# A decode step with adaptive norms, cached attention and a token mixer: the last eight heads in an order written out step by step

## The chip, the cores and the metric

The kernel runs on one core of a Trainium2 chip. The metric is device time in microseconds (us) of the whole program, the median of several runs. Engines are named as the profile names them: PE is TensorE's matmuls and PEld its weight loads, DVE is VectorE, ACT is ScalarE, POOL is GpSimd, SP is SyncE, which here only issues DMAs. All data is float32.

## The reference, cut to what matters

One token for each of four batch rows goes through an attention block with cached keys and values and then through a token mixer, each behind an adaptive layer norm.

```python
mod = (silu(c) @ w_mod).reshape(4, 6, 1, 512)       # w_mod: 512 x 3072
sa, ca, ga, sb, cb, gb = ...                        # the six blocks of it
h = layernorm(x) * (1 + ca) + sa                    # x: 4 x 1 x 512
q = h @ wq                                          # 32 heads of 128
scores = q @ k.T * 128 ** -0.5                      # 8 key/value heads, 4096 keys, 4 query heads on each
o = softmax(scores) @ v
x = x + ga * (o @ wo)
h = layernorm(x) * (1 + cb) + sb
u = gelu(layernorm(h)[:, :, None] * w1 + b1)        # per channel: 1 -> 1792
x = x + gb * (u @ w2 + b2)                          # 1792 -> 1
```

The keys and values are 4 x 8 x 4096 x 128 each, 67 MB and 67 MB; with the weights about 157 MB are read.

## The kernel before, in words

Work is counted in rounds 0 to 31, one for each pair of batch row and key/value head (round 8b + h). The host has laid out the keys of a round as 128 x 4096 and its values as 128 partitions of 32 rows of 128.

**Loads.** SP issues all loads. A ring of three slots, each with room for two blocks of 2 MB, holds them: `load_pair(i)` brings the keys of round i+2 and the values of round i in one DMA of 4 MB. The last slots are filled block by block: the keys of rounds 30 and 31 (`load_key`), the values of 28 and 29, the values of 30 and 31 in pieces (`load_v`), and at the end the sixth block of `w_mod` (`load_wm5`, L206). A load waits until every reader of what stood in its slot is done.

**A round.** The steps of round i, each with its engine:

- scores (PE, L238): eight products of 32 columns of queries with 512 keys each, into `s`, a PSUM tile of 128 x 1024; then DVE takes the row maximum (L241).
- the maximum over the four row groups: PE turns it (L247), DVE reduces it (L249), PE spreads it (L256), DVE copies it (L258).
- exponential on ACT with row sums (L261).
- transposes: PE turns the exponentials into the same PSUM tile `s` (L268), PE adds the row sums (L272); DVE copies the turned values to `pT` (L276; L274 for round 31) and makes from the sums a selecting matrix (L279, L281).
- values (PE, L292; L302 for round 31): 16 products with 256 value columns each, accumulated in `pv`; DVE copies them (L296, L306).
- project: PE picks the query heads from that copy (L317), DVE copies them (L319), PE multiplies with `wo` (L328 or, for the last batch row, L335), DVE adds to the row's sum (L342, L344). Rounds 30 and 31 add into the tile `pgx` instead.

`s` has two buffers, `pv` one, and one more PSUM pool of two buffers serves every small result in turn (turned maximum, spread maximum, sums, pick, project, gathered statistics): a new one waits until the reader of the one two before it is done.

**The mixer.** When a batch row's eight rounds are done, the class `Mixer` does its second half piecemeal in the next rounds: `residual`, two norms (statistics on DVE, gathered over partitions by PE at L369), `normalise`, then seven pieces each of `expand` (DVE, L405), `gelu` (ACT, L448) and `consume` (PE, L410 or L416). The last batch row's mixer is `finish`, at the end of the program. `fold_gate` multiplies (DVE, L537) two of `wo`'s blocks with the residual's gate so that rounds 30 and 31 can add straight to the residual.

**The order.** The program is given in `manual_schedule`: every engine runs its instructions in the order in which Python emits them, and waits are derived from the tiles. Rounds 0 to 27 come from one loop, in which round i does scores i+2, pick i-1, transposes i+1, project i-1, the maximum i+2, values i in two halves, the exponential i+2 and a part of the mixer. Rounds 28 to 31 follow in straight code (L589 to L639), ending in the residual of the last batch row and `finish`.

Of the kernel before, what the change touches and what calls it, by code (L numbers as in the profile page):

```python
# [19 lines left out]
P = 128  # L20
# [11 lines left out]
def adaln_decode(ctx: ExitStack, tc: tile.TileContext, small, x, wmod, wq, kk, kv, vv, wo, out):  # L32
# [20 lines left out]
    nc.sync.dma_start(sm, small)  # L53
# [177 lines left out]
    S, SEL, SP = {}, {}, {}  # L231

    def scores(i):
        b, h = divmod(i, HKV)
        s = ps_s.tile([P, 1024], F32, name=f"s{i}", tag="s")
        for n in range(2):
            for c in range(4):
                mm(s[32 * c:32 * c + 32, n * 512:(n + 1) * 512], QT[:, b, h, :],  # L238
                   KT[i][:, (n * 4 + c) * 512:(n * 4 + c + 1) * 512], start=True, stop=True)
        m = wk.tile([P, 1], F32, name="m")  # L240
        dv.tensor_reduce(m, s, axis=AX.X, op=OP.max)  # L241
        S[i] = [s, m]

    def colmax(i):
        s, m = S[i]
        pm = ps_m.tile([1, P], F32, name="pm", tag="m")
        nc.tensor.transpose(pm, m, ident)  # L247
        mx = wk.tile([1, 4, 32], F32, name="mx")
        dv.tensor_reduce(mx, pm.rearrange("o (c r) -> o r c", c=4).unsqueeze(1).to_broadcast([1, 4, 32, 4]),  # L249
                         axis=AX.X, op=OP.max)  # L250
        S[i] = [s, mx]

    def expo(i):
        s, mx = S[i]
        pb = ps_m.tile([P, 1], F32, name="pb", tag="m")
        mm(pb, mx.rearrange("o c r -> o (c r)"), neg1, start=True, stop=True)  # L256
        nm = wk.tile([P, 1], F32, name="nm")
        dv.tensor_copy(nm, pb)  # L258
        p = wk.tile([P, 1024], F32, name="p", tag="p")
        l = wk.tile([P, 1], F32, name="l")  # L260
        nc.scalar.activation(p, s, AF.Exp, bias=nm, accum_out=l)  # L261
        S[i] = [s, p, l]

    def transposes(i, then=None):
        s, p, l = S.pop(i)
        pt = s.rearrange("p (k n) -> p k n", k=8)
        for k in range(8):
            nc.tensor.transpose(pt[:, k, :], p[:, k * P:(k + 1) * P], ident)  # L268
        if then:
            then()  # L270
        pl = ps_m.tile([P, 1], F32, name="pl", tag="m")
        mm(pl, grp, l, start=True, stop=True)  # L272
        if i == NS - 1:
            dv.tensor_copy(pTl[:, :, :, 0:REP], pt.rearrange("p k (c r) -> p k c r", c=4)[:, :, :, 0:REP])  # L274
        else:
            dv.tensor_copy(pTs[i % 3][:, :, 0:2 * REP].rearrange("p k (c r) -> p k c r", c=2),  # L276
                           pt.rearrange("p k (h c r) -> p (k h) c r", h=2, c=2)[:, :, :, 0:REP])
        rl = wk.tile([P, 1], F32, name="rl")
        dv.reciprocal(rl, pl)  # L279
# [4 lines left out]
    PV = {}  # L284

    def values(i, ks, pv=None):
        if ks[0] == 0:
            PV[i] = ps_v.tile([P, 2 * DH], F32, name="pv", tag="pv") if pv is None else pv
        pv = PV[i]
        for k in ks:  # L290
            q = k % 4
            mm(pv[32 * q:32 * q + 32, :], pTs[i % 3][:, k, :],  # L292
               VT[i][:, k * 2:(k + 1) * 2, :].rearrange("p j d -> p (j d)"), start=(k < 4), stop=(k >= 12))
        if ks[-1] == 15:
            po = wk.tile([P, 2 * DH], F32, name="po")
            dv.tensor_copy(po, pv)  # L296
            SP[i] = (SEL.pop(i), po)

    def values_last(i, ks, pv):
        for k in ks:  # L300
# [3 lines left out]
        if ks[-1] == 7:  # L304
            po = wk.tile([P, DH], F32, name="po")
            dv.tensor_copy(po, pv)  # L306
            SP[i] = (SEL.pop(i), po)

    ACC = {}
    OT = {}  # L310

    def project_a(i):
        sel, po = SP.pop(i)
        pt = ps_m.tile([P, REP], F32, name="pt", tag="m")
# [3 lines left out]
        oT = wk.tile([P, REP], F32, name="oT")  # L318
        dv.tensor_copy(oT, pt)  # L319
        OT[i] = oT  # L320

    def project_b(i, pa=None):
# [7 lines left out]
        else:  # L330
# [7 lines left out]
            if h >= HKV - 2:  # L338
                return
        if h == 0:  # L340
# [78 lines left out]
    class Mixer:  # L419
# [5 lines left out]

        def residual(self):
            b = self.b
            residual(XK[:, b], fold_groups(ps_e, ACC.pop(b), "e"))
            self.st = stats(XK[:, b], b)

        def modulate(self):
            self.h1, self.st = adaln(self.b, gather(self.st))

        def normalise(self):
            self.hb, self.wr = affine(gather(self.st), bcast(self.h1, self.b))
# [34 lines left out]
        def inner(self, k):  # L470
            self.ripe = len(self.done)
            if k == 0:
# [201 lines left out]
```

## Time and profile before

| | us |
|---|---|
| runs shown | 393.55, 395.03, 395.13 |
| median | 395.03 |
| profiled execution, whole | 393.89 |
| its span, first to last instruction | 392.1 |
| PE busy | 298.3 (76%) |
| DVE busy | 180.3 (46%) |
| ACT busy | 99.6 (25%) |
| time of the load queue's packets, share of 16 DMA engines | 93.6% |
| bytes moved | 157.80 MB |

The busy time of an engine is a sum over stages with different limits. The span has three parts: the prologue (modulation and queries) until the first keys are there, the rounds, and the end behind the last load. Which engine or queue sets the pace is read from each part by itself, by what ended the waits in it.

### The profile page before, as it was taken

The page shows a single profiled execution, that of the slowest core. Times are in us where ns is not written, and L with a number is a line of the kernel's source. Part 1 is how long each engine was busy: PE and PEld are TensorE (multiplying, and loading weights), DVE is VectorE, ACT ScalarE, POOL GpSimd, SP SyncE. Part 2 cuts the span into 40 slices and gives each one's busy share as a digit, 9 for nine tenths or more (in the row PEclk, how much of TensorE's full clock was granted, in tenths as well). Part 3 has the DMA queues.
Part 4 walks back from the last instruction along what each step waited for, and adds up shares of the span by engine and source line. Part 5 has one row for each costly group of instructions (what it writes and reads, how often), then busy time and mean ns, then how long its engine had stood idle before and what let it go on. Part 6 is the DMA issues. An engine that isn't in the chain of part 4 may idle for free.

```text
span 392.1 us, 7228 instructions
## 1 busy us (share of the span) xinstructions
PE 298.3 (76%) x3180; PEld 146.8 (37%) x3180; DVE 180.3 (46%) x491; ACT 99.6 (25%) x123; POOL 0.7 (0%) x6
## 2 busy tenths in 40 slices
PE   0578685913868739978698879998888879899885
PEld 0012142400533305434243325553334225555663
DVE  0620331510433404666365524765555356557766
ACT  1001120110110201114548111145751111465316
POOL 0000000000000000000000000000000000000000
PEclk9989886985998957999899976999999889999997
DMA  8999999999999999999999999999999999999600
GB/s 325 428 431 431 428 453 440 404 448 431 425 431 426 436 426 438 433 440 439 426 431 424 430 435 430 433 428 434 436 435 430 431 430 430 416 425 420 258 3 3
DMA packets 7415, 157.80 MB, mean 402 GB/s; under 512 B 964, under 2 KB 980, under 8 KB 1368
## 3 DMA queue, kind: packets, MB, share of 16 engines
q1 hardware_dynamic: 7376, 157.33, 93.6%
q8 instruction: 25, 0.41, 0.4%
q14 instruction: 6, 0.05, 0.0%
q10 hardware_dynamic: 8, 0.00, 0.0%
HBM read 157.32 MB, written 0.01 MB: 401 GB/s over the span
## 4 chain that ended last, share of the span: by engine, by line
DMA 64%; PE 27%; DVE 6%; ACT 1%; issue 1%; SPq 0%; DVEq 0%
DMA kv<-in_kv 57%; PE s L238 7%; DMA kv<-in_vv 5%; PE pv L292 3%; PE pa L328 3%; PE s L268 3%; PE s L137 2%; PE qs L152 2%; DMA sm<-in_small 2%; PE pt L317 2%; DVE mx L249 1%; PE py L410 1%; DVE acc L344 1%; PE pb L256 1%; PE pm L223 1%
## 5 line engine op out<-in xcount | busy, mean ns | idle before, releaser
L238 PE MATMUL s<-kv,QT 128*32 128x512 f32 x512 | 76.5, 725 | 55.0 <-DMA kv<-in_kv 54.6
L261 ACT ACTIVATE p<-s,nm 128x1024 f32<-128x1024 f32 x32 | 35.7, 1115 | 212.9 <-DVE nm L258 212.8
L241 DVE TENSOR_REDUCE m<-s 128x1 f32<-128x1024 f32 x32 | 39.2, 1225 | 104.9 <-PE s L238 104.8
L292 PE MATMUL pv<-kv,pT 128*32 128x256 f32 x960 | 64.5, 387 | 0.0
L238 PEld LDWEIGHTS s<-kv,QT 128*32 128x32 f32 x512 | 15.6, 123 | 94.8 <-DMA kv<-in_kv 62.4
L268 PE MATMUL s<-ident,p 128*128 128x128 f32 x256 | 36.5, 288 | 0.6 <-ACT p L261 0.6
L268 PEld LDWEIGHTS s<-ident,p 128*128 128x128 f32 x256 | 31.5, 157 | 3.7 <-ACT p L261 1.9
L292 PEld LDWEIGHTS pv<-kv,pT 128*32 128x32 f32 x960 | 25.6, 110 | 15.3 <-issue 0.6
L317 PEld LDWEIGHTS pt<-sel,po 128*128 128x128 f32 x126 | 17.6, 202 | 30.8 <-issue 25.7
L328 PE MATMUL pa<-wo,oT 128*32 128x512 f32 x192 | 27.3, 642 | 0.0
L249 DVE TENSOR_REDUCE mx<-pm 1x128 f32<-1x512 f32 x32 | 21.5, 672 | 0.7 <-PE pm L247 0.7
L317 PE MATMUL pt<-sel,po 128*128 128x4 f32 x126 | 20.3, 266 | 1.1 <-DVE po L296 1.0
L448 ACT ACTIVATE u<-u 128x1024 f32<-128x1024 f32 x20 | 20.3, 1051 | 2.2 <-DVE u L405 2.1
L405 DVE TENSOR_SCALAR u<-hb,wr,sm 128x512 f32<-128x512 f32 x40 | 19.9, 540 | 1.9 <-PE py L416 1.9
L137 PE MATMUL s<-wm,sT 128*4 128x512 f32 x16 | 9.6, 770 | 14.3 <-DVE sT L123 14.3
L344 DVE TENSOR_TENSOR acc<-acc,pa 128x512 f32<-128x512 f32 x21 | 14.5, 688 | 11.3 <-PE pa L328 11.3
L296 DVE COPY po<-pv 128x256 f32<-128x256 f32 x30 | 12.7, 423 | 11.8 <-PE pv L292 11.8
L261 ACT ACT_TABLE_LOAD x9 | 11.5, 1283 | 25.6 <-DVE nm L258 25.5
L256 PEld LDWEIGHTS pb<-neg,mx 1*128 1x128 f32 x64 | 9.4, 182 | 20.0 <-DVE mx L249 20.0
L256 PE MATMUL pb<-neg,mx 1*128 1x1 f32 x64 | 12.1, 256 | 5.9 <-DVE mx L249 5.9
L448 ACT ACT_TABLE_LOAD x11 | 14.1, 1283 | 0.2
L276 DVE COPY pT<-s 128x128 f32<-128x128 f32 x31 | 9.0, 291 | 9.9 <-PE s L268 9.2
(142 smaller groups left out, 231.1 us busy)
## 6 DMA issues: line engine op xcount, KB each, us to landing
kv<-in_kv SPq DMA_DIRECT2D x28, 4096.0 KB, 21.6
wq<-in_wq SPq DMA_DIRECT2D x2, 4096.0 KB, 16.3
wo<-in_wo SPq DMA_DIRECT2D x4, 2048.0 KB
kv<-in_kv SPq DMA_DIRECT2D x3, 2048.0 KB, 17.4
wm<-in_wmod SPq DMA_DIRECT2D x2, 2048.0 KB, 16.1
kv<-in_kk SPq DMA_DIRECT2D x1, 4096.0 KB
kv<-in_vv SPq DMA_DIRECT2D x3, 1024.0 KB
kv<-in_kv SPq DMA_DIRECT2D x2, 1024.0 KB, 17.6
```

What stands on the lines that cost most here:

```text
L238: mm(s[32 * c:32 * c + 32, n * 512:(n + 1) * 512], QT[:, b, h, :], KT[i][:, (n * 4 + c) * 512:(n * 4 + c + 1) * 512], start=True, stop=True)
L241: dv.tensor_reduce(m, s, axis=AX.X, op=OP.max)
L249: dv.tensor_reduce(mx, pm.rearrange("o (c r) -> o r c", c=4).unsqueeze(1).to_broadcast([1, 4, 32, 4]), axis=AX.X, op=OP.max)
L256: mm(pb, mx.rearrange("o c r -> o (c r)"), neg1, start=True, stop=True)
L261: nc.scalar.activation(p, s, AF.Exp, bias=nm, accum_out=l)
L268: nc.tensor.transpose(pt[:, k, :], p[:, k * P:(k + 1) * P], ident)
L292: mm(pv[32 * q:32 * q + 32, :], pTs[i % 3][:, k, :], VT[i][:, k * 2:(k + 1) * 2, :].rearrange("p j d -> p (j d)"), start=(k < 4), stop=(k ...
L317: mm(pt, po[:, c * DH:(c + 1) * DH], sel[:, c * REP:(c + 1) * REP], start=(c == 0), stop=(c == n - 1))
L328: mm(pa[32 * g:32 * g + 32, :], oT[:, g:g + 1].to_broadcast([P, 32]), wo_t[h][:, g, :], start=True, stop=True)
L344: dv.tensor_add(ACC[b], ACC[b], pa)
L405: dv.tensor_scalar(u[:, e, :], hb, wr[:, j:j + 1], b1[:, j:j + 1], op0=OP.mult, op1=OP.add)
L448: nc.scalar.activation(u, u, AF.Gelu_apprx_tanh)
```

## The change

The functions of a round are cut into steps that each emit work for one engine: `scores`, `row_max`, `turn_max`, `col_max`, `spread_max`, `copy_max`, `expo`, `turn`, `sums`, `copy_p`, `scale`, `values` (now in quarters of four products), `copy_v`, `pick`, `copy_o`, `project`, `add_up`. `Mixer` gets `fold`, `gather` and `spread` as steps of their own, and the head of `finish` becomes steps of a second `Mixer`. The loop now ends after round 23 and calls the steps in the order in which it did before. The rest is one list, `PLAN`, of some 200 entries: a letter for a step and the round, with the quarter behind a point for values. Besides, the table `small` (128 rows of 236 bytes) is loaded in three DMAs instead of one.

```diff
-    nc.sync.dma_start(sm, small)
+    for lo, hi in ((0, 6), (6, 16), (16, P)):
+        nc.sync.dma_start(sm[lo:hi], small[lo:hi])
...
-    def colmax(i):
-        s, m = S[i]
+    def row_max(i):
+        M[i] = wk.tile([P, 1], F32, name="m")
+        dv.tensor_reduce(M[i], S[i], axis=AX.X, op=OP.max)
+
+    def turn_max(i):
         pm = ps_m.tile([1, P], F32, name="pm", tag="m")
-        nc.tensor.transpose(pm, m, ident)
+        nc.tensor.transpose(pm, M[i], ident)
+        M[i] = pm
...
+    def spread_max(i):
+        pb = ps_m.tile([P, 1], F32, name="pb", tag="m")
+        mm(pb, M[i].rearrange("o c r -> o (c r)"), neg1, start=True, stop=True)
+        M[i] = pb
...
-    nc.scalar.activation(tab, neg1, AF.Exp)
-    n = NS - 4
-    load_v(t[:, 1], n + 1, (0, 16, 32))
-    project_a(n - 1)
-    project_b(n - 1)
-    scores(n + 2)
-    transposes(n + 1)
...
-    project_a(n + 3)
-    project_b(n + 3, x3)
-    finish(B - 1, pgx[:, 0], x3, mix)
+    mix, row = Mixer(B - 2), Mixer(B - 1)
+    pve = pgx = ep = spare = slot = None
+    gates = list(range(2 * REP))
+    cuts = {NS - 1: (0, 16, 24, 28, 32), NS - 2: (0, 16, 32)}
+    last = [(0, 1, 2, 3), (4, 5), (6,), (7,)]
+    PLAN = """
+    a23 A23 s26 p23 v24.0 S26 m26 v24.1 P23 F t25 X26 LP25 v24.2 v24.3 R G b26 V24 C25 v25.0 M B26 e26
+    LP26 a24 s27 A24 v25.1 p24 S27 v25.2 v25.3 m27 f P24 l25 L25 V25 X27 t26 C26 H b27 Q N x a25 s28
+    v26.0 B27 A25 v26.1 S28 e27 g x LP27 m28 X28 t27 b28 LT C27 l26 L26 v26.2 B28 p25 x v26.3 c LK30 l27
+    P25 g V26 x e28 a26 T c s29 L27 t28 v27.0 f A26 S29 m29 v27.1 v27.2 X29 b29 C28 B29 l28 f s30 LK31
+    e29 v27.3 f f t29 S30 g C29 L28 V27 LT p26 P26 LV28 m30 s31 X30 a27 LV29 A27 b30 p27 B30 S31 c v28.0
+    P27 l29 v28.1 v28.2 L29 e30 m31 v28.3 V28 t30 X31 a28 LT A28 b31 p28 x B31 v29.0 f LV30 C30 v29.1 x
+    e31 v29.2 g l30 v29.3 LV31 L30 g v30.0 P28 V29 t31 f LW l31 a29 v30.1 L31 v30.2 g C31 v30.3 Y A29
+    p29 v31.0 V30 f x v31.1 a30 A30 v31.2 P29 v31.3 V31 p30 a31 E A31 I p31 zs c g zg c zx zm c c zg zb
+    zn zw0 zc zw1
+    """
+    TABLE = {"s": scores, "S": row_max, "m": turn_max, "X": col_max, "b": spread_max, "B": copy_max, "e": expo,
+             "t": turn, "l": sums, "C": copy_p, "L": scale, "V": copy_v, "a": pick, "A": copy_o, "P": add_up,
+             "LP": load_pair}
+    MIX = {"F": mix.fold, "R": mix.residual, "G": mix.gather, "M": mix.modulate, "H": mix.gather, "Q": mix.spread,
+           "N": mix.normalise, "g": mix.gelu, "c": lambda: mix.consume(1), "zc": mix.close, "zg": row.gather,
+           "zm": row.modulate, "zn": row.normalise}
+    for step in PLAN.split():
...
+        elif op == "v":
+            if i == NS - 1:
+                values_last(i, last[q], pve[:, 1, 0:DH])
+                continue
...
+        elif op == "p":
+            project(i, pgx[:, 4] if i >= NS - 2 else None)
...
+        elif op == "x":
+            mix.expand(spare if mix.n == 6 else None)
+        elif op == "f":
+            fold_gate(gate, gates[:1])
+            del gates[:1]
+        elif op == "T":
+            nc.scalar.activation(tab, neg1, AF.Exp)
...
+        elif op == "E":
+            ep = cst.tile([P, P], F32, name="ep")
+            residual(ep, ACC.pop(B - 1))
+        elif op == "I":
+            mm(pgx[:, 4], ident, ep, start=False, stop=False)
+        elif op == "zs":
+            row.st = stats(pgx[:, 4], B - 1)
...
+    finish(B - 1, pgx[:, 0], py[:, 0], row.hb, row.wr)
```

Of the other entries, `LT` takes the next slot of the ring, `LP`, `LK`, `LV` and `LW` issue the loads of pairs, keys, values and the sixth modulation block into it, `Y` takes the tile `pgx`, `zx` copies the residual, `zb` spreads the normed row, and `zw` multiplies the sixth modulation block.

More of the change, by code (lines that the diff above doesn't have):

```diff
@@ L542, in adaln_decode @@
     for i in range(2):
-        scores(i)
-        colmax(i)
-        expo(i)
-    transposes(0)
+        for step in (scores, row_max, turn_max, col_max, spread_max, copy_max, expo):
+            step(i)
+    for step in (turn, sums, copy_p, scale):
+        step(0)
     mix = None
-    for i in range(NS - 4):
-        if i < NS - 5:
-            load_pair(i + 1)
-        else:
-            t = slots()
-            load_key(t[:, 0], NS - 2)
-            load_key(t[:, 1], NS - 1)
-            t = slots()
-            load_v(t[:, 0], i + 1, (0, 32))
+    for i in range(NS - HKV):
+        load_pair(i + 1)
         if i in (1, 3, 5):
@@ L561, in adaln_decode @@
         scores(i + 2)
+        row_max(i + 2)
         if i:
-            project_a(i - 1)
-        transposes(i + 1)
+            pick(i - 1)
+            copy_o(i - 1)
+        turn(i + 1)
+        sums(i + 1)
+        copy_p(i + 1)
+        scale(i + 1)
         if i:
-            project_b(i - 1)
-        colmax(i + 2)
+            project(i - 1)
+            add_up(i - 1)
+        turn_max(i + 2)
+        col_max(i + 2)
         values(i, range(8))
+        spread_max(i + 2)
+        copy_max(i + 2)
         expo(i + 2)
@@ L573, in adaln_decode @@
             mix.inner(i % HKV)
-            if i == NS - HKV:
-                fold_gate(gate, (0, 1))
         values(i, range(8, 16))
+        copy_v(i)
         if mix:
@@ L588, in adaln_decode @@
             gate = spread_gate()
-    nc.scalar.activation(tab, neg1, AF.Exp)
-    n = NS - 4
-    load_v(t[:, 1], n + 1, (0, 16, 32))
-    project_a(n - 1)
-    project_b(n - 1)
-    scores(n + 2)
-    transposes(n + 1)
-    colmax(n + 2)
-    mix.consume()
-    expo(n + 2)
-    mix.expand()
-    scores(n + 3)
-    transposes(n + 2)
-    colmax(n + 3)
-    values(n, range(8))
-    expo(n + 3)
-    mix.gelu()
-    mix.both()
-    values(n, range(8, 16))
-    fold_gate(gate, (2,))
-    t = slots()
@@ L610, in adaln_decode @@
-    load_v(t[:, 0], n + 2, (0, 16, 32))
-    transposes(n + 3, lambda: project_a(n))
-    project_b(n)
-    mix.both()
-    fold_gate(gate, (3,))
-    values(n + 1, range(16))
-    load_v(t[:, 1], n + 3, (0, 16, 24, 28, 32))
-    spare = load_wm5()
-    pve = ps_s.tile([P, 2, 512], F32, name="pve", tag="s")
-    fold_gate(gate, (4, 5))
-    values(n + 2, range(8), pve[:, 0, 0:2 * DH])
-    project_a(n + 1)
-    project_b(n + 1)
-    mix.both(spare)
-    values(n + 2, range(8, 16))
-    pgx = ps_s.tile([P, 8, P], F32, name="pgx", tag="s")
@@ L626, in adaln_decode @@
-    x3 = pgx[:, 4]
-    project_a(n + 2)
-    ep = cst.tile([P, P], F32, name="ep")
-    residual(ep, ACC.pop(B - 1))
-    fold_gate(gate, (6, 7))
-    pvl = pve[:, 1, 0:DH]
-    values_last(n + 3, range(0, 4), pvl)
-    project_b(n + 2, x3)
-    for ks in ((4, 5), (6,), (7,)):
-        values_last(n + 3, ks, pvl)
-    mm(x3, ident, ep, start=False, stop=False)
-    project_a(n + 3)
-    project_b(n + 3, x3)
-    finish(B - 1, pgx[:, 0], x3, mix)
+    mix, row = Mixer(B - 2), Mixer(B - 1)
+    pve = pgx = ep = spare = slot = None
```

150 lines of the change are left out of this document (83 added, 67 removed).

## The prediction

> **What bounds the kernel now.** I read the busy times by stretch first, then the DMA issues with their time to landing, then the chain of waits, and the timeline where the chain cannot be believed. Of the stretches, PE is TensorE's matmuls, PEld its weight loads, DVE VectorE, ACT ScalarE; PEclk is the granted clock.
>
> ```profile
> core 0 of [0], span 392.1 us
> core 0: us, PE busy (x) PEld busy (x) DVE busy (x) ACT busy (x) POOL busy (x), PEclk, DMA share, GB/s
> 0.00:10.00 10.00, 0.00 (x0) 0.00 (x0) 0.97 (x8) 1.50 (x2) 0.70 (x6) 1.00 0.85 322
> 10.00:20.00 10.00, 5.73 (x8) 0.95 (x9) 5.94 (x19) 0.00 (x0) 0.00 (x0) 1.00 1.01 436
> 20.00:30.00 10.00, 7.33 (x30) 1.84 (x31) 2.33 (x4) 0.00 (x0) 0.00 (x0) 0.83 1.03 446
> ...
> 340.00:350.00 10.00, 9.52 (x157) 6.11 (x161) 5.76 (x16) 4.78 (x5) 0.00 (x0) 1.00 1.00 426
> 350.00:360.00 10.00, 9.59 (x120) 5.19 (x110) 6.63 (x16) 5.45 (x8) 0.00 (x0) 1.00 1.00 422
> 360.00:370.00 10.00, 8.03 (x151) 5.92 (x148) 6.81 (x19) 5.42 (x7) 0.00 (x0) 1.00 0.86 353
> ```
>
> The 16 DMA engines are full from the start until after 360 us, so the loads run at their own pace and an order of the engines can't shorten them; it can only stop them from being issued. What an order can change lies at the end: how soon after the last landing the result is there.
>
> When does the last load land? The issue queue and the table of issues (KB, median us to landing) say:
>
> ```profile
> 23.92 0.33 SPq L184 DMA_DIRECT2D kv<-in_kk  x1
> ...
> 356.93 0.33 SPq L206 DMA_DIRECT2D kv<-in_wmod  x1
> ```
>
> ```profile
> kv<-in_wmod SPq DMA_DIRECT2D x1, 1024.0 KB, 14.7
> ...
> sm<-in_small SPq DMA_DIRECT2D x1, 29.5 KB, 7.6
> ```
>
> The sixth modulation block is issued last, at 356.93, and lands at 371.6. It is 1.05 MB, 2.4 to 2.5 us at 422 to 426 GB/s, so the last quarter MB of values 31 lands at 369.2. Counting back by bytes at that rate: the other pieces of values 31 land at 368.6, 368.0 and 366.7, values 30 at 364.2 and 361.7, values 29 by 359.3, values 28 at 354.3, key 31 (8.4 MB before the end of values 31) at 349.5, key 30 at about 344.6.
>
> Now the chain of waits (start, us, what):
>
> ```profile
> 290.08 1.92 PE s L238 x16
> 292.00 0.54 PE pt L317 x4
> 292.54 0.93 PE s L268 x8
> 293.47 0.12 PE pl L272 x2
> 293.59 1.04 PE pa L328 x8
> ...
> 320.62 3.23 PE s L238 x16
> ...
> 326.65 1.00 PE pv L292 x16
> ...
> 368.41 1.00 DVE kv L405 x2
> ...
> 369.79 0.61 PE pt L317 x4
> 370.40 1.01 PE pve L302 x32
> 371.41 0.87 PE pgx L335 x32
> 372.29 0.87 PE pve L302 x32
> 373.16 0.42 PE pgx L636 x2
> 373.58 0.39 PE pt L317 x2
> ...
> 374.21 1.12 PE pgx L335 x32
> ...
> 375.36 0.31 DVE st L361
> ```
>
> The chain steps from L405 straight to a DMA. I don't believe that step: the block that L405 writes is not what was being loaded. What was late is seen in the timeline:
>
> ```profile
> 349.40 1.90 PE L238 MATMUL s<-kv,QT 128*32 128x512 f32 x16
> ...
> 363.15 1.91 PE L292 MATMUL pv<-kv,pT 128*32 128x256 f32 x32
> ```
>
> The scores of head 30 start at 349.40, 4.8 us after their key has landed. The values of head 29 start at 363.15, 3.8 us after the last of them has landed. The first values of head 31 start at 370.40, 3.7 us after landing. TensorE lags the loads by almost 4 us through the last five heads, because the list makes it wait for VectorE and ScalarE (its idle time is 10 minus busy: 0.48, 0.41 and 1.97 us in the three stretches). The token's residual is complete at 375.36; from there to the end of the span are 16.7 us of a chain in which each step needs the one before.
>
> **The change, part by part.**
>
> *The new list up to the last values.* No arithmetic is added or removed in the eight rounds; they are the old steps, cut finer and set in another order. So the sum is the new TensorE list laid against the landings, with start-to-start times from the chain: scores 1.92, pick 0.54, turn 0.93, sums 0.12, project 1.04, a quarter of values 0.50 (half of 1.00). Row maximum's turn and its spread are not on the chain as I quote it; between the 0.12 of a small product and the 0.54 of a pick I take 0.25. One consumed mixer piece is 8 matmuls of the project's narrow shape, half of 0.87 to 1.04, so 0.5.
>
> - From key 31 (349.5): scores 31, pick 27, spread 30, project 27, consume: 1.92+0.54+0.25+1.04+0.5 = 4.25, so 353.8; wait for values 28 until 354.3.
> - values 28 with sums 29 and turned maximum 31: 2.0+0.12+0.25, to 356.7. Turn 30, pick 28, spread 31, project 28: 2.76, to 359.4. Values 29 and sums 30: 2.12, to 361.5.
> - values 30.0 (361.7), turn 31, sums 31, pick 29, values 30.1: 2.59, to 364.3; values 30.2 and 30.3: 365.3; project 29: 366.3.
> - values 31.0 (366.7): 1.0, to 367.7; 31.1 (368.0) 0.5, to 368.5; pick 30, 369.0; 31.2, 369.3; 31.3 (369.2) to 369.6.
> - project 30, which now stands behind all values: 0.87 to 1.04, to 370.5. Its place costs about 0.35, as the copy of values 31 (0.3) and its hand-over end earlier. Pick 31 to the start of project 31 takes 374.21 − 373.58 = 0.63, in which the residual's product (0.42) is hidden; project 31 to the statistics 1.15: 372.3.
>
> The list has 0.4 us to spare before values 31.0 and 0.3 before 31.1; whatever else is late arrives in the sum. Lower bound: no lag, 372.3. Upper bound: the old lag, 375.4. Near the lower end, because the new list takes each block within 0.5 us of its landing, where the old one first queued turn, project and two consumed pieces; I add 0.3 and take 372.6, a gain of **2.8 us**.
>
> A cold clock earlier: the new list has the values of head 25 in front of pick 24 and scores 27, so TensorE waits there for pair 25, until about 320.6, as scores 27 do now. After a wait, scores took 3.23 (row 320.62) where others took 1.92; the same 1.3 us is lost there as now, a round of 9.6 us ahead of the next pair, and the waits at 354.3 and 361.7 take it up. The Trainium skill (TensorE: Matmul & The Clock Gate, Part 1) says that a window of about 3.4 us without work halves the clock, and that a busy one restores it. By that rule the loss might be longer there, an estimated 3.4 us of half speed or 1.7 us lost; the end would be the same by both, since the list has caught up by 366.
>
> *VectorE beside it.* In the list stand a gate fold and an expansion between copy of values 30 and copy of pick 30. The expansion is 1.00 (row 368.41); the fold is of the same shape at half the count, so 0.5 to 1.0. They are hidden behind values 31.1, pick 30 and 31.2; without that cover they'd cost up to 2. The old list had the expansion (row 368.41) in front of the copy of values 30, and pick 30 waited for both: that is one of the stalls removed, and late next is TensorE itself.
>
> *Issue of the loads.* Pairs and blocks are issued in the same order; only the releases of the three slots move. The first half of values 30 needs scores 29 and values 27, which the new list ends behind scores 30 (344.6 + 1.92 + 0.5 = 347.1). At that time values 28 and 29 are still in the queue, until 359.3: 12 us of cover. Cost nothing; if the release were over 10 us late the DMA engines would run dry.
>
> *The small table in three loads.* SyncE issues two more, each 0.33 to 0.4 (row 23.92 has 0.33), so the table is complete 0 to 0.9 us later. It opens the chain that ends in the first scores' modulation and the issue of the first keys at 23.92. What still covers that issue are the 10.5 MB of modulation and query blocks ahead of it: 3.2 and 4.4 MB are done by 20 us (322 and 436 GB/s), the other 2.9 MB at 446 GB/s last until 26.5. So up to 0.9 us is hidden behind some 2.5. I take 0; without the cover it would be 0.9 on everything.
>
> *The finish.* One consumed piece (0.5) now stands between project 31 and the gathering of statistics; VectorE's 0.5 for the statistics hide it but for about 0.1. The bias of the third mixer is added behind the last norm, 0.3 on VectorE, in front of expansions that ScalarE waits for only after its first two activations. Together 0 to 0.4, taken 0.1.
>
> **Sum.** 392.1 − 2.8 + 0.1 = 389.4 of span. The profiled execution took 393.89 in all, 1.8 outside the span, so 391.2. It lies 1.1 under the median of the runs shown (395.03); from that the same 2.7 gives 392.3. I forecast **391.8**. What a measurement can tell from no change is 0.5%, 2 us.
>
> **Rivals.**
>
> 1. *Half of the lag stays.* Score maxima, sums, picks and projects share two buffers, so each new one waits for the VectorE reader of the one two before; an expansion (1.00) stands in front of the copy of maximum 31, whose exponential gates turn 31, in front of most of values 30. For it: VectorE is busy 6.6 to 6.8 of 10. Against: by my sum that exponential is done more than 1 us ahead of turn 31. If it holds, values 30.1 and all behind are about 1.5 us later: 393.3, no telling change.
> 2. *Slower: the price of the pieces.* From scores 29 to values 31.0 the TensorE list has 41 pieces, each with its own hand-over. The sum takes start-to-start times that hold the hand-overs of the old list only. If each new piece costs 0.2 more, that is 8 us, less about 2 of waits that it fills: the residual at 378.3, 3 us later than now, 398. It decides from about 0.12 a piece. For it: values now come in quarters between small products. Against: picks, sums and transposes (0.54, 0.12, 0.93) already stand back to back on the chain without such a gap.
> 3. *A cold clock at the end.* Scores took 3.23 at 320.62, after a wait for their key, where others took 1.92. If TensorE ran the last values, project 30, pick 31 and project 31 (2.4 us) at such a rate, 2 us of the gain go: 393.8, no telling change. Against it: the longest wait of my sum behind key 31 is 0.5 us, and the granted clock is 1.00 from 340 to 370 us. The rule of the Trainium skill quoted above would ask for a wait of some 3.4 us just there.
> 4. *The loads end earlier or the finish shortens* by another 2 us, through something in the three small loads that I don't see: 389.5. Nothing in the rows speaks for it.
> 5. *The order has no effect*, because a wait the compiler derives (slot, buffer) holds the old order: 395.0. Against it, the old stalls sit in the list itself.
>
> **Chances.** Forecast 0.66 (391 to 393), rival 1 0.14, rival 2 0.07, rival 3 0.03, rival 4 0.05, rival 5 0.05. The forecast's own spread and half of rival 1 go up to 394.2; with rival 4 the range is 389.6 to 394.4. Faster by over 0.5% (under 393.05): most of the forecast, rival 4 and a third of rival 1: 0.75. Within: 0.17. Slower: 0.08.
>
> **What would show it.** Right: values 31's first product starts within 1 us of 366.7, the statistics of the residual at 372 to 373, and from there 16.6 to 16.9 us to the end; the last modulation block still lands at about 371.6; DMA share unbroken. Wrong: that product still at 370 (rivals 1, 2), the granted clock under 1 between 360 and 373 (rival 3), a DMA share under 0.9 before 365 us, or the finish longer than before.

## The result, and the profile after

| | before | after |
|---|---|---|
| median, us (9 runs each, side by side) | 393.69 | 391.49 |
| lowest to highest | 393.55 to 396.54 | 391.21 to 393.54 |
| profiled execution, whole | 393.89 | 391.32 |
| its span | 392.1 | 389.4 |
| first product of values 31 | 370.33 | 366.41 |
| statistics of the residual | 375.36 | 372.43 |

The ratio of the times is 0.994, with a 95% interval of 0.9915 to 0.9964: the kernel became about 0.6% faster, a small change but one clear of the scatter. The forecast was 391.8 us with a span of 389.4, and the statistics at 372.6.

The busy times by stretch of the new kernel (columns as in the prediction: PE, PEld, DVE, ACT and POOL busy, granted clock, DMA share, GB/s):

```profile
320.00:330.00 10.00, 9.78 (x99) 5.18 (x99) 4.25 (x13) 1.21 (x2) 0.00 (x0) 0.69 0.99 426
...
340.00:350.00 10.00, 10.00 (x129) 5.46 (x132) 7.49 (x17) 4.18 (x7) 0.00 (x0) 1.00 1.01 429
350.00:360.00 10.00, 10.00 (x172) 6.54 (x168) 5.70 (x17) 2.56 (x4) 0.00 (x0) 1.00 0.99 419
360.00:370.00 10.00, 9.45 (x196) 6.86 (x192) 6.13 (x20) 5.84 (x7) 0.00 (x0) 1.00 0.86 356
```

TensorE has no idle time left between 340 and 360 us (10.00 and 10.00, where it had 9.52 and 9.59), and 0.55 instead of 1.97 between 360 and 370. The DMA share is what it was: the loads run as before, only TensorE follows them closer. The timeline of the new kernel (start, duration, engine, line, operation, tiles; in brackets an idle time and what ended it) shows the slow scores 27, scores 30, and the way from values 31 to the statistics:

```profile
320.22 1.08 PE L303 MATMUL pv<-kv,pT 128*32 128x256 f32 x8 [1.83 <-DVE h L395]
...
322.17 3.64 PE L239 MATMUL s<-kv,QT 128*32 128x512 f32 x16
...
346.02 1.92 PE L239 MATMUL s<-kv,QT 128*32 128x512 f32 x16
...
366.41 1.08 PE L310 MATMUL pve<-kv,pTl 128*32 128x128 f32 x32
367.56 0.42 DVE L316 COPY po<-pve 128x256 f32<-128x256 f32 x1 [3.09 <-PE pve L310]
...
368.04 0.64 PE L310 MATMUL pve<-kv,pTl 128*32 128x128 f32 x16 [0.55 <-DVE po L316]
...
372.43 0.30 DVE L373 BATCH_NORM_STATS2 st<-pgx 128x6 f32<-128x128 f32 x1 [1.21 <-PE pgx L345]
```

The trace records when the last of the 16 DMA engines has finished each load. Set against the first product that reads it:

| block | before: landed, read, lag | after: landed, read, lag |
|---|---|---|
| key 30 | 344.86, 349.40, 4.5 | 344.52, 346.02, 1.5 |
| key 31 | 349.59, 354.16, 4.6 | 349.32, 350.54, 1.2 |
| values 28 | 354.44, 357.63, 3.2 | 354.19, 354.59, 0.4 |
| values 29 | 359.31, 363.15, 3.8 | 359.02, 359.81, 0.8 |
| values 30, first half | 361.81, 364.88, 3.1 | 361.49, 361.98, 0.5 |
| values 31, first half | 366.66, 370.33, 3.7 | 366.37, 366.41, 0.0 |

The last quarter MB of values 31 lands at 369.24 before and at 368.82 after. From there to the statistics of the residual it is **6.12 us before and 3.61 after**: the order gives 2.51, and 0.42 come from the earlier landing. The change didn't move the loads: taken as the mean over the 16 DMA engines, that piece lands at 366.68 before and at 366.80 after, and only the engine that finishes last is earlier. The end behind the statistics is 392.12 − 375.36 = 16.76 before and 389.42 − 372.43 = 16.99 after. The table of DMA issues (KB, median us to landing) has the last two pieces, which were issued at 351.29 and 351.76:

```profile
kv<-in_vv SPq DMA_DIRECT2D x2, 256.0 KB, 17.1
```

Profiled executions with the same loads land them up to 1.9 us apart (what goes with it is told at the end). So beside each kernel's time stands the time from the landing of the last piece of values 31 to the statistics, in which that is left out. Here it is for all that was run, under the names that the experiments below explain; each ratio is to runs of the kernel before beside it, whose median lay between 393.69 and 394.06 us:

| kernel | median us (runs), ratio to before [95%] | span | last piece lands | statistics | between |
|---|---|---|---|---|---|
| before | 393.69 (9) | 392.1 | 369.24 | 375.36 | 6.12 |
| after | 391.49 (9), 0.994 [0.9915, 0.9964] | 389.4 | 368.82 | 372.43 | 3.61 |
| old_late | 394.08 (10), 1.0008 [0.9976, 1.0039] | 391.9 | 372.47 | 375.14 | 2.67 |
| new_late | 395.74 (10), 1.0029 [0.999, 1.0068] | 392.0 | 371.49 | 375.06 | 3.57 |
| new_head_old_tail | 393.58 (10), 0.9972 [0.994, 1.0003] | 391.9 | 368.88 | 374.96 | 6.08 |
| old_head_new_tail | 398.74 (4), 1.0119 [1.006, 1.0179] | 396.8 | 368.97 | 379.80 | 10.83 |
| old_head_new_tail2 | 394.47 (10), 1.0011 [0.9979, 1.0042] | 392.0 | 370.23 | 374.98 | 4.75 |
| old_head_new_tail3 | 397.43 (10), 1.0068 [1.0036, 1.0099] | 393.2 | 369.74 | 376.22 | 6.48 |
| old_head_new_tail4 | 392.02 (12), 0.9939 [0.9908, 0.997] | 390.0 | 369.03 | 373.04 | 4.01 |
| new_halves | 392.06 (12), 0.9946 [0.9924, 0.9968] | 389.7 | 368.92 | 372.70 | 3.78 |
| new_table_whole | 391.39 (7), 0.9932 [0.9903, 0.9962] | 390.7 | 370.36 | 373.86 | 3.50 |
| own_bank | 391.81 (11), 0.9929 [0.9907, 0.9952] | 390.8 | 370.72 | 373.81 | 3.09 |
| own_bank_pick | 391.79 (7), 0.993 [0.9904, 0.9956] | 389.2 | 368.97 | 372.25 | 3.28 |
| new_again | 391.64 (10), 0.9929 [0.9902, 0.9955] | 389.6 | 368.93 | 372.63 | 3.70 |

### The profile page after: what moved, and what is told of

The parts are those of the page before. It is cut to its first block, busy times and chain, and to the rows that moved or that the text cites. A ratio compares the mean times of both kernels' runs of the same rounds, so it can differ in the third digit from the quotient of the medians.

```text
span 389.4 us, 7234 instructions
## 1 busy us (share of the span) xinstructions
PE 299.0 (77%) x3180; PEld 147.7 (38%) x3180; DVE 180.0 (46%) x491; ACT 99.4 (26%) x123; POOL 0.7 (0%) x6
## 4 chain that ended last, share of the span: by engine, by line
DMA 53%; PE 36%; DVE 7%; ACT 2%; issue 1%; SPq 0%; DVEq 0%
DMA kv<-in_kv 51%; PE s L239 10%; PE pv L303 6%; PE s L274 4%; PE pa L338 3%; PE pt L325 2%; PE s L138 2%; DMA sm<-in_small 2%; PE qs L153 2%; PE pq L345 1%; DVE mx L253 1%; ACT uu L523 1%; PE pb L259 1%; DVE acc L356 1%; PE pl L278 1%
## 5 line engine op out<-in xcount | busy, mean ns | idle before, releaser
L239 PE MATMUL s<-kv,QT 128*32 128x512 f32 x512 | 77.3, 731 | 49.5 <-DMA kv<-in_kv 48.6
L303 PE MATMUL pv<-kv,pT 128*32 128x256 f32 x960 | 66.4, 391 | 1.8 <-DVE h L395 1.8
L325 PEld LDWEIGHTS pt<-sel,po 128*128 128x128 f32 x126 | 18.4, 210 | 27.0 <-issue 23.5
L338 PE MATMUL pa<-wo,oT 128*32 128x512 f32 x192 | 28.1, 661 | 0.0
L248 PEld LDWEIGHTS pm<-ident,m 128*1 128x1 f32 x32 | 2.5, 79 | 30.3 <-DVE sel L293 17.2
```

Source lines behind the costliest of these rows:

```text
L303: mm(PV[i][32 * q:32 * q + 32, :], pTs[i % len(pTs)][:, k, :], VT[i][:, k * 2:(k + 1) * 2, :].rearrange("p j d -> p (j d)"), start=(k < 4) ...
L325: mm(pt, po[:, c * DH:(c + 1) * DH], sel[:, c * REP:(c + 1) * REP], start=(c == 0), stop=(c == n - 1))
L338: mm(pa[32 * g:32 * g + 32, :], oT[:, g:g + 1].to_broadcast([P, 32]), wo_t[h][:, g, :], start=True, stop=True)
```

## Experiment 1: load the last values later

If the old order lags the loads by almost 4 us, those loads can come 2.5 us later without any cost; if the new order has caught up, the same delay costs it 2.5 us. Both kernels get the sixth modulation block (1 MB, not needed until the end) ahead of values 31. In the old kernel:

```diff
-    load_v(t[:, 1], n + 3, (0, 16, 24, 28, 32))
     spare = load_wm5()
+    load_v(t[:, 1], n + 3, (0, 16, 24, 28, 32))
```

In the new list the entry `LW` goes in front of `LV31`.

> The old order, with the sixth modulation block (1 MB, needed last) loaded ahead of the values of round 31 instead of behind them. Nothing else is changed; the last quarter MB of values 31 should land at about 371.6 us instead of 369.2. Theory (the old TensorE list runs 3.7 us behind the loads when it reaches values 31, and the new one runs with them): no cost, since the first product of values 31 starts at 370.4 anyway and the last at about 373: statistics of the residual at 375.4 to 375.7, span 392.1 to 392.5. Rival (the end simply follows the last landing in both orders, and the gain came from something else): statistics at 377.8, span 394.5.

> The new order with the same exchange of the last two loads: the sixth modulation block ahead of values 31. Theory (the new list waits for values 31): the whole 2.4 us are paid: first product of values 31 at about 368.8 instead of 366.4, statistics at 374.8 instead of 372.4, span 391.7 to 391.9, as long as the old order. Rival (in the new order TensorE's list is the bound and the landing only happens to be near): at most 1 us, statistics by 373.4, span by 390.4.

The first products of values 31 and the statistics in the timeline of the old order with late values, and behind it the first products in the new order with the same:

```profile
370.10 1.08 PE L302 MATMUL pve<-kv,pTl 128*32 128x128 f32 x32
...
375.14 0.30 DVE L361 BATCH_NORM_STATS2 st<-pgx 128x6 f32<-128x128 f32 x1 [1.20 <-PE pgx L335]
```

```profile
369.06 1.08 PE L310 MATMUL pve<-kv,pTl 128*32 128x128 f32 x32 [2.22 <-DMA kv<-in_vv]
```

In the old order the last piece landed at 372.47 instead of 369.24, and the statistics stayed where they were (375.14 against 375.36), the time too (1.0008). In the new order TensorE stands still for 2.22 us until the load is there; it landed 2.67 later than in the new kernel and the statistics are 2.63 later. The old order was bound by TensorE's list, the new one is bound by the last landing. The times point the same way, but the exchange cost the new order more in them than in the profile: a ratio of 1.0029 instead of 0.994, some 3.5 us, with runs from 393.85 to 399.05. The profiled execution (393.93) is among the fastest, so what the others add isn't seen in it.

One thing more can be read here. With the loads late enough, the old order needs 2.67 us from the last landing to the statistics, the new one 3.57. The new end behind the last load is 0.9 longer than the old one; the gain of the order comes in spite of it (experiment 4).

## Experiment 2: which part of the list does it

The list is cut in two: the steps that belonged to the rounds of heads 24 to 27, and the rest. One half at a time is put back into the old order (shortened; letters as in the program's table):

```diff
 # new_head_old_tail: the first half as in the new list, then
+    T LV29 a27 A27 p27 P27 s30 S30 t29 l29 C29 L29 m30 X30 c c b30 B30 e30 x s31 S31 ...
 # old_head_new_tail: the rounds as the old loop had them, the last of them
+    s29 S29 a26 A26 t28 l28 C28 L28 p26 P26 m29 X29 v27.0 v27.1 b29 B29 e29 x g v27.2 v27.3 V27 c x g
 # and then the rest as in the new list
+    x T c f s30 f f t29 S30 C29 m30 s31 X30 a27 LV29 A27 b30 p27 B30 S31 c v28.0 ...
```

> The complement: the steps that the old loop has in rounds 24 to 27 in the new list's order, and behind them the old order of the rest (the small table in three loads). Theory (both parts are needed): values 31 start about 1.3 us earlier than in the old order, statistics at about 374.1, span about 390.8. Rival 1 (the last four rounds do it all): statistics at 375.4, span 392.1. Rival 2 (the first four rounds do it all): 372.4, span 389.4.

> Steps of the loop's rounds 24 to 27 in the old order, and behind them the other steps of the list in the new order (the small table in three loads as in the new kernel). Theory (the lag builds up over all eight rounds, as TensorE in the old order of rounds 24 to 27 leaves steps undone that it could do while it waits for keys): a part only: laid out by the rows of the trace, values 31 start 0.9 us earlier than in the old order, statistics at about 374.5, span about 391.2. Rival 1 (the order of the last four rounds does it all): statistics at 372.4, span 389.4. Rival 2 (the first four do it all): 375.4, span 392.1.

The second expectation failed in all its versions: 398.74 us, slower than both kernels. Of the first, the theory failed as well (statistics at 374.96, not 374.1), and its first rival came out: the new head with the old tail gave 0.04 us between landing and statistics (6.08 against 6.12). Its timeline shows the lag forming again at scores 30, whose key landed at 344.61:

```profile
348.12 1.08 PE L345 MATMUL pq<-wo,oT 128*32 128x128 f32 x32 [0.25 <-DVE oT L330]
...
349.01 1.90 PE L239 MATMUL s<-kv,QT 128*32 128x512 f32 x16
```

All of values 27, pick 27 and project 27 stand in front of scores 30, as in the old list. Through the rounds before, a key lands about every 9.7 us (329.74 and 339.49 for keys 28 and 29 in the new kernel), and such a place costs nothing. Keys 30 and 31 follow 5 us apart, without values between them, and there it costs 4.5 us. The new list has the last quarter of values 27 behind scores 30, and pick 27 and project 27 behind scores 31.

And the old head with the new tail (the second `c`, one consumed piece of the mixer, is the row of L422):

```profile
351.39 1.08 PE L422 MATMUL py<-u,sm 128*32 128x128 f32 x16 [3.76 <-ACT u L468]
...
352.25 2.79 PE L239 MATMUL s<-kv,QT 128*32 128x512 f32 x12
```

TensorE waits 3.76 us in front of scores 30 for a piece whose gelu is still to come, since the old rounds had not got that far, and then runs scores 30 slow (2.79 for twelve products, where sixteen take 1.9). So this mix measured its own seam. The next kernel moves that piece behind project 27:

```diff
-    x T c f s30 f f t29 S30 C29 m30 s31 X30 a27 LV29 A27 b30 p27 B30 S31 c v28.0
+    x T f s30 f f t29 S30 C29 m30 s31 X30 a27 LV29 A27 b30 p27 B30 S31 c c v28.0
```

> Old order in the rounds of heads 24 to 27, new order behind it, with the one consumed piece that stood in front of scores 30 (and waited 3.76 us there for its gelu) moved behind project 27. What the list itself can do is then judged without that wait. Theory (the lag is made and avoided in the order of the last four heads): scores 30 within 2 us of 346.0, first product of values 31 at 366.4 to 366.9, residual's statistics at 372.4 to 372.9, span 389.4 to 389.9. Rival (both parts are needed, the rounds of heads 24 to 27 must leave no work over): scores 30 still at 348 to 350, statistics 374 to 375, span 391 to 392. Second rival (the earlier run was slow for another reason than that wait): statistics again near 379.8, span 396.8.

```profile
347.54 1.90 PE L239 MATMUL s<-kv,QT 128*32 128x512 f32 x16
347.69 1.91 DVE L417 TENSOR_SCALAR u<-hb,wr,sm 128x512 f32<-128x512 f32 x4
...
349.51 1.89 DVE L548 TENSOR_TENSOR wo<-wo,gate 128x512 f32<-128x512 f32 x3
...
352.59 0.27 PE L248 MATMUL pm<-ident,m 128*1 128x128 f32 x1 [2.13 <-DVE m L244]
```

Scores 30 come at 347.54, but VectorE first does two expansions and three gate folds that the old rounds left over, and takes row maximum 30 only behind them, 3.8 us after scores 30 began; the turn of that maximum, and scores 31 behind it, wait 2.13 us. By the statistics and the span (374.98 and 392.0) this was the rival's result. But again it is leftover work in the way, and so the next kernel takes the maximum first:

```diff
-    x T f s30 f f t29 S30 C29 m30 s31 ...
+    T s30 S30 x f f f t29 C29 m30 s31 ...
```

> Old order in the rounds of heads 24 to 27, new order behind, with two moves: no consumed piece stands in front of scores 31, and VectorE takes row maximum 30 straight behind scores 30, before the expansion and the three gate folds that the old rounds leave over (in the mix before, VectorE worked 5 us on two expansions and three folds ahead of that maximum, and scores 31 waited 2.13 us for it). Judged by the time from the landing of the last quarter MB of values 31 to the residual's statistics: 6.12 us in the old order, 3.61 in the new, 4.75 in the mix before. Theory A (the rounds of heads 24 to 27 matter only through the work of VectorE and the consumed pieces that they leave for the next ones): 3.6 to 4.0 us, statistics near 372.6 if the loads land as in the new kernel, span 389.6. Theory B (TensorE itself comes out of the old rounds too late, with values 27 and project 27 still to do): 4.5 to 5, span 390.5 to 391.

```profile
351.89 1.89 DVE L548 TENSOR_TENSOR wo<-wo,gate 128x512 f32<-128x512 f32 x3
...
354.03 1.92 PE L239 MATMUL s<-kv,QT 128*32 128x512 f32 x16 [2.64 <-DVE pT L286]
```

A miss for both theories: 6.48. The same expansion and folds now stand in front of the copy of turned values 29. `s` has two buffers, so scores 31 wait for that copy: 2.64 us. The work had only been moved from one reader that gates scores 31 to the other. The last of these kernels puts it behind scores 31:

```diff
-    T s30 S30 x f f f t29 C29 m30 s31 X30 a27 LV29 A27 b30 p27 B30 S31 c c v28.0 P27 l29
+    T s30 S30 t29 C29 m30 s31 X30 a27 LV29 A27 b30 p27 B30 x f S31 c c v28.0 P27 f f l29
```

> Old order in the rounds of heads 24 to 27 and new order behind, but every expansion and gate fold that the old rounds leave over stands behind scores 31 on VectorE, and the consumed pieces behind project 27. In the mix before, scores 31 waited 2.64 us for a copy that stood behind one expansion and three folds. Theory A (the old rounds harm only through the work of VectorE that they leave over): scores 31 at 350.3 to 351.3, landing of the last quarter MB to statistics 3.6 to 4.2 us, span 389.5 to 390.3, time within 0.2% of the new kernel's. Theory B (whatever is left over is late somewhere, because VectorE has no 3 us to spare between scores 30 and values 31): scores 31 early, but row maximum 31, turn 31 and the first values of 31 late; 4.7 us or more, span over 390.8, no telling gain over the kernel before.

```profile
347.12 1.90 PE L239 MATMUL s<-kv,QT 128*32 128x512 f32 x16
...
350.85 1.92 PE L239 MATMUL s<-kv,QT 128*32 128x512 f32 x16 [0.21 <-DVE pT L286]
```

Theory A came out: scores 31 at 350.85, 4.01 between landing and statistics, 392.02 us (0.14% over the new kernel's 391.49). So (6.12 − 4.01) / 2.51 = 84% of the gain is had with the old order up to head 27 and the new one behind it, **if** VectorE's leftovers stand behind scores 31. The new order of the first four heads brings nothing alone; what it does in the whole is to leave VectorE free in time. In the new kernel the last expansion ahead of scores 30 starts at 339.77 and takes 1.00, and three folds run while TensorE does scores 30 (346.02), ahead of row maximum 30:

```profile
345.89 1.88 DVE L548 TENSOR_TENSOR wo<-wo,gate 128x512 f32<-128x512 f32 x3
```

## Experiment 3: the quarters and the small table

The values of heads 24 to 30 are put back into halves, each at the place of its first quarter (one line of the list is shown):

```diff
-    e31 v29.2 g l30 v29.3 LV31 L30 g v30.0 P28 V29 t31 f LW l31 a29 v30.1 L31 v30.2 g C31 v30.3 Y A29
+    e31 v29.2 v29.3 g l30 LV31 L30 g v30.0 v30.1 P28 V29 t31 f LW l31 a29 L31 v30.2 v30.3 g C31 Y A29
```

> The new order, with the values of heads 24 to 30 in halves as before, each at the place of its first quarter (the quarters of head 31 stay). Theory (what counts is that no product stands in front of work whose load has landed; values in one piece or two cost little): statistics within 0.4 of 372.43, span 389.3 to 389.9. Rival (the quarters make the gain, because a half of values hides a small product's way over VectorE only once): the lag comes back by half, statistics 373.5 to 374.5, span 390.5 to 391.5.

3.78 against 3.61 and 3.70 in the two profiles of the new kernel: the quarters are worth 0.1 to 0.2 us, which the times (0.9946 against 0.994) don't show.

The small table in one load again:

```diff
-    for lo, hi in ((0, 6), (6, 16), (16, P)):
-        nc.sync.dma_start(sm[lo:hi], small[lo:hi])
+    nc.sync.dma_start(sm, small)
```

> The new order, with the small table loaded by one transfer as before instead of three. Theory (its split costs and brings nothing: the issue of the first keys at 23.97 against 23.92 before): last landing of values 31 at 368.8 within 0.2, span 389.2 to 389.7, time as the new kernel's. Rival (the values of the last head landed 0.4 us earlier than in the kernel before because of the split): they land at 369.2, span 389.8, time 0.4 us over the new kernel's.

The time is the new kernel's, 391.39. In this profile the last piece landed at 370.36, which neither theory expected; it is one of the late executions told of at the end, so the last landing can't tell whether the split moved the loads by a few tenths. The first keys can: with one load they were issued at 22.99 and landed at 28.12, in the new kernel at 23.97 and 28.10. The split neither costs nor brings anything that the times show.

## Experiment 4: what the end behind the last load still holds

In the timeline of the new kernel above, the copy of values 30 (367.56) waits for the first products of values **31**, and the second products of values 31 (368.04) wait 0.55 us for that copy, though their load had landed at 367.58. The two don't share data: values 30 are in the first half of the tile `pve`, values 31 in the second, 2 KB apart. But it is one tile, and its waits are made for the whole of it. The old kernel has the same tile. In the next kernel values 31 get a tile from the other pool:

```diff
-                values_last(i, last[q], pve[:, 1, 0:DH])
+                if q == 0:
+                    pvl = ps_v.tile([P, 2 * DH], F32, name="pv", tag="pv")[:, 0:DH]
+                values_last(i, last[q], pvl)
```

> The new order unchanged; only the last head's values are added up in a buffer of the other pool instead of the second half of the tile whose first half holds the values of head 30. Theory (the two halves of that one tile are ordered against each other: the copy of values 30 waits for the first products of 31, and the second products of 31 wait for that copy): the copy of values 30 starts right after values 30's last product, before the first of values 31 ends (about 0.9 us earlier than 367.56), values 31.1 no longer waits for VectorE, pick 30 stands earlier, statistics 0.3 to 0.6 us earlier (371.8 to 372.1 against 372.43), span 388.8 to 389.1. Rival (the last quarter MB, landing at 368.82, sets the end anyway, and what stands behind it is the same): statistics within 0.15 of 372.43, span 389.3 to 389.6.

```profile
367.21 0.42 DVE L316 COPY po<-pve 128x256 f32<-128x256 f32 x1 [1.22 <-PE pve L303]
...
368.34 1.76 PE L310 MATMUL pv<-kv,pTl 128*32 128x128 f32 x48 [0.32 <-DMA kv<-in_vv]
```

The copy of values 30 now comes before the first product of values 31 and right behind values 30's last, and no product of values 31 waits for VectorE. The numbers expected for the statistics were missed, as the loads of this execution landed 1.9 us later; between landing and statistics it is 3.09, 0.5 to 0.6 less than in the new kernel's two profiles. Up to 0.2 of that may be due to the late loads (the late profile of experiment 3 has 3.50). The times (0.9929 against 0.994 and 0.9929 for the new kernel) can't show half a microsecond.

The next kernel also moves pick 30 and project 30 forward, and the residual ahead of the copy of values 31; the last one is the new kernel again, unchanged:

```diff
-    p29 v31.0 V30 f x v31.1 a30 A30 v31.2 P29 v31.3 V31 p30 a31 E A31 I p31
+    p29 V30 a30 v31.0 P29 A30 f v31.1 p30 x E v31.2 v31.3 V31 a31 A31 I p31
```

> The last head's values in a tile of the other pool, and, since the copy of values 30 is then early, pick 30 in front of the first values of 31 and project 30 in front of the last two pieces, the residual before the copy of values 31 on VectorE. Judged from the landing of the last quarter MB to the residual's statistics: 3.61 us in the new kernel, 3.09 with the tile alone. Theory (project 30's 0.9 us of TensorE between values 31 and pick 31 is the next thing on the path): 2.7 to 2.85 us, span 388.6 to 388.8 where the loads land as in the new kernel, time 0.7 to 0.8 us under the new kernel's. Rival (pick 31 waits for VectorE's copy anyway, and VectorE's expansion, fold and residual now stand in front of it): 3.1 or more, no gain over the tile alone.

> The new kernel once more, unchanged, on the same chip as the two beside it, since the landing of the last values of 31 moved by up to 1.9 us from one execution to another (368.8 to 370.7) without any change to the loads. Theory (the end follows the landing): landing to statistics 3.5 to 3.7 us whatever the landing is, time 391.2 to 392 us. Rival (the time from landing to statistics depends on when the loads land): it comes out shorter than 3.4 where the loads are late.

```profile
367.22 1.52 PE L310 MATMUL pv<-kv,pTl 128*32 128x128 f32 x48
...
369.42 0.62 PE L310 MATMUL pv<-kv,pTl 128*32 128x128 f32 x16
```

and of its stretches:

```profile
360.00:370.00 10.00, 10.00 (x224) 7.67 (x212) 6.92 (x23) 6.41 (x7) 0.00 (x0) 1.00 0.86 353
```

The theory failed: 3.28 instead of 2.7 to 2.85. The rival's number came out, but not for its reason: VectorE waits for the last product before it copies values 31, not the other way round. Pick 30 now delays the first values of 31 (367.22, landed at 366.48), and project 30 (368.55) stands in front of the last two pieces, which had landed at 368.34 and 368.97 and run at 369.42. TensorE is simply full between 360 and 370 us (10.00 of 10.00 in this kernel), and a step moved forward pushes another back by its length. The new kernel run again gave 3.70 and 391.64; its loads were not late, so it doesn't tell whether late loads shorten that time. No version beats the new kernel by more than the runs can tell.

## Why the prediction was right, step by step

**The bound.** "The loads run at their own pace", and TensorE lags them by almost 4 us: shown by experiment 1, where a later load cost the old order nothing and the new one all of it. The reason given for the lag, that the list makes TensorE "wait for VectorE and ScalarE", is only half of it. In the kernel before, TensorE stands still for just 0.48 of the 4.5 us between the landing of key 30 (344.86) and scores 30 (349.40). It is busy with what the list has in front of them, values 27, a consumed piece, pick 27 and project 27:

```profile
345.90 1.07 PE L292 MATMUL pv<-kv,pT 128*32 128x256 f32 x16
...
347.52 0.61 PE L317 MATMUL pt<-sel,po 128*128 128x4 f32 x4
...
348.50 1.08 PE L335 MATMUL pq<-wo,oT 128*32 128x128 f32 x32 [0.37 <-DVE oT L319]
...
369.79 0.61 PE L317 MATMUL pt<-sel,po 128*128 128x4 f32 x4 [0.97 <-DVE po L296]
```

The waits, 2.38 us between scores 30 and values 31, keep the lag from shrinking. The new order shortens the first part (scores 30 are 1.5 behind) and takes out the second (no idle time from scores 30 to values 31).

**The landings** counted back by bytes were those of the old kernel within 0.3 us (369.2 for 369.24, 366.7 for 366.66, 354.3 for 354.44, 349.5 for 349.59, 344.6 for 344.86). In the new kernel they came 0.25 to 0.4 earlier. This was not forecast (rival 4 speaks of such a thing, at 2 us). It lies with the engine that finishes last: the mean over the 16 engines differs by 0.12 us at most between the two profiles at each block of the table, and old_late, whose order and loads are the old ones up to values 30, has key 30 at 344.52 like the new kernel. Why that engine finishes earlier in one execution than in another stays open.

**The list against the landings.** Lower bound 372.3, taken 372.6, measured 372.43. The sum lets scores 31 start with their key; they came at 350.54, 1.2 behind it, and the waits and the slack that the sum had further on took this up. Then: values 31.0 forecast at 366.7 (with the landing), measured 366.41; 31.1 at 368.0 and 368.04; project 30 at 369.6 and 369.62. That these agree to a few hundredths is luck, as two errors cancel. The landings were 0.4 earlier, but 31.1 did not wait for its load, landed at 367.58; it waited 0.46 longer for the copy of values 30 (experiment 4). The working had read the two halves of `pve` as independent. Project 30 behind all values was priced at 0.35; with the wait just named that would be 0.8 of the 0.9 by which the new end is longer in experiment 1; no run measures the place of project 30 alone.

**VectorE beside it.** The fold and the expansion were hidden as said: project 30 starts at 369.62, right behind the last values. What the prediction did not see is how much hangs on VectorE's order further up, ahead of scores 31: experiment 2 lost 0.7 to 2.5 us there (4.75 and 6.48 between, against 4.01) by leftover expansions and folds in the wrong place.

**The issue of loads.** The release of values 30 was put at 347.1; it came at 348.44. With 12 us of cover it cost nothing, and the DMA share is unbroken.

**The cold clock** at head 25 was there and was larger: scores 27 took 3.64 (3.23 before), the clock granted between 320 and 330 was 0.69, and scores 28 started 2.1 us after their key had landed (331.86, 329.74) instead of at once. The half clock (0.50) lasted 6.83 us there, from 319.46, against 3.41 before; TensorE worked for some 6.1 of them, so that about 3 us were lost, an estimate from these rows, 1.72 of it in scores 27 (3.64 − 1.92). The estimate that the prediction worked out from the Trainium skill (TensorE: Matmul & The Clock Gate, Part 1), 3.4 us of half speed and 1.7 us lost, was too small; and TensorE had been idle for 1.1 us when the clock fell, and for 1.83 in all (row 320.22), about half of the 3.4 us without work that the Trainium skill asks for there. "The waits at 354.3 and 361.7 take it up" held: TensorE did not wait there, and the lag fell from 1.5 to 1.2 and then to 0.4 at values 28.

**The finish** was priced at +0.1. From the statistics to the third mixer's normed row (`hb`) it takes 5.15 us, 5.10 before. From there to the end of the span it is 11.84, before 11.66. The last store is issued 9.27 behind that row, before 9.26, and lands 1.57 later in both; so 0.17 of the difference lie behind the last landing, where the program closes (1.00 us, before 0.83, and 0.89 with the small table in one load), and the finish itself cost 0.05.

**The rivals.** Half of the lag staying (1): no, 0.0 at values 31. The price of the pieces (2): none; the list met its landings with all 41 pieces, and quartering moved 0.1 to 0.2. A cold clock at the end (3): the granted clock is 1.00 from 340 to 373 (the price of 2 us was high: 2.4 us at 3.23 for 1.92 are 1.6 more). No effect of the order (5): no, the lag at values 31 went from 3.7 to 0.0.

**The basis.** The forecast lies between 391.2 (from the profiled execution) and 392.3 (from a median of 395.03 over three runs). With nine runs that median is 393.69; the profiled execution was the better basis. That 391.8 came within 0.3 of the 391.49 is in part luck: the gain was 2.7 in the spans, as forecast, but 2.2 in the medians, and a start that was too high makes up for it.

## What to carry to other kernels

Lay the instruction list of the busiest engine against the landings of the loads: a lag in front of the last blocks is the gain that an order can have, and loading a late block still later shows on the chip whether it is there. Where the rhythm of the loads changes (here two keys in a row 5 us apart, after one every 9.7), the order that fitted the loop needs its own list, and a small step of another engine in front of the wrong reader costs as much as the whole list brings. Once the engine is full, moving its steps forward only trades one delay for another; look for waits between things that share no data, as between two halves of one tile.

## What was not expected

**How long the clock stays low early on goes with how late the last load lands.** The first product after a wait of 13 to 15 us for key 5 is at about 95 us in every profile. In the new kernel's profile TensorE is back at full speed behind that one row of scores; in that of the kernel with values 31 in their own tile it is slow for some 9 us, and the next load, which waits for the values of that round, is issued 3.7 us later (1.0 of it because that key had landed later already). The new kernel:

```profile
94.72 3.32 PE L239 MATMUL s<-kv,QT 128*32 128x512 f32 x16 [14.73 <-DMA kv<-in_kv]
...
98.44 1.07 PE L274 MATMUL s<-ident,p 128*128 128x128 f32 x8
...
103.46 4.19 SPq L191 DMA_DIRECT2D kv<-in_kv  x2
```

```profile
100.00:110.00 10.00, 8.97 (x165) 5.32 (x158) 3.92 (x9) 1.21 (x2) 0.00 (x0) 1.00 1.04 444
```

and values 31 in their own tile:

```profile
95.76 3.64 PE L239 MATMUL s<-kv,QT 128*32 128x512 f32 x16 [14.53 <-DMA kv<-in_kv]
...
100.21 1.95 PE L274 MATMUL s<-ident,p 128*128 128x128 f32 x8
...
107.16 4.19 SPq L191 DMA_DIRECT2D kv<-in_kv  x2
```

```profile
100.00:110.00 10.00, 9.17 (x123) 5.64 (x127) 3.80 (x11) 1.21 (x2) 0.00 (x0) 0.75 0.94 380
```

By then the load queue has run nearly dry: 380 GB/s instead of 444 in that stretch. In 14 profiles that load is issued at 103.3 to 103.9 us nine times, and the last load of the program lands at 371.3 to 371.6; five times it is issued at 105.7 to 107.2, and the last load lands at 372.2 to 373.1. Both happen with the old order and with the new one. The profile's record of the granted clock divides them in the same way: around that wait the half clock lasts 13.65 us in the nine and 17.07 or 20.48 in the five, that is four, five or six times 3.41. And the delay stays: taken as the mean over the 16 DMA engines, the landings from that load on to the values of 28 differ from the new kernel's by at most 0.2 us in the other eight of the nine, and by about 0.3, 0.4, 0.7, 0.8 and 1.5 us throughout in the five. (The last of the 16 engines, by which the tables here go, scatters by half a microsecond more.) This may well be the spread of the new kernel's runs (391.2 to 393.5); that was read from the traces, and no run was made to test it. The Trainium skill (TensorE: Matmul & The Clock Gate, Part 1) says that the window of about 3.4 us by which the clock is set runs freely, so that the number of slow products differs from run to run, and puts the loss at under 1% of a typical kernel. The steps of 3.41 us agree with the first, and 0.9 to 1.9 us of 391 in the last landing with the second; but that is as much as the whole change brings, and a comparison of two single profiles would have been off by it.
